# Order of the first loads in a one-token attention and gated-MLP kernel: both halves of the gate weights ahead of the input x

## The chip, the cores and the metric

The kernel runs on one core of a Trainium2 chip. The metric is the device time of one execution in microseconds (us), as the median of several runs. Before the change it is 198.14 us (three runs, 198.09 to 198.21).

The engines named here: TensorE (PE; its weight loads are PEld), VectorE (DVE), ScalarE (ACT), GpSimd (POOL) and SyncE (SP). Transfers between the chip's memory (HBM) and the on-chip SBUF are done by 16 DMA engines. A transfer is put to them by an instruction on SP's queue or on ACT's queue. PSUM is the memory that TensorE writes its sums to.

## What is computed

Eight tokens x (8 x 512, bf16) go through a layer norm. The result feeds an attention over the last 2048 positions of a key and value cache (32 query heads, 8 key/value heads, 128 wide), and a gated MLP that is used as a gate:

```python
xn = _layernorm(x)
# A: attention over the last W = 2048 positions of the caches
q = (xn @ wq), split into 32 heads
p = _softmax(einsum("bhqd,bhkd->bhqk", q, k) * Dh ** -0.5)
s = einsum("bhqk,bhkd->bhqd", p, v) @ wo
# B: the gate
h = _sigmoid(xn @ w_gate) * (xn @ w_up)
g = _silu(h @ w_down)
return x + s * g
```

(The heads' reshapes are left out.) Nearly all the bytes are the two caches, 16 loads of 2 MB each for keys and for values, and the weights: w_gate, w_up and w_down 1.8 MB each, wq and wo 4 MB each; 81 MB in all.

## The kernel before

**Loads.** Nothing is computed without a load, and the loads are put in one long order. A list `todo` holds them with the pool that each needs (k, v or d; L111 to L130), and `pump` (L114) issues from its front as long as the pool has room; `free` (L120), called behind the work that used a tile, gives the room back and issues on. Almost all go on SP's queue (`q0`). In order: `want_first` (L151) with the gate weights and x; w_up (L169); wq in two halves (L205); w_down (L207) and its small remainder `wd_part` in two transfers (L188 to L203); then for each of 16 pairs of token and group of four key heads the keys (from L211) and, three places later, the values; at the end wo in five pieces (L216 to L223). The pool for keys has four tiles, and wq's halves take two of them at first, so the third load of keys waits until the first half of wq has been used. Of `want_first`, four transfers: x as 8 rows of 512 (`x_bf`, L153) on SP's queue; the gate weights (`wg_sb`, L155) in two halves of 896 KB, the first on ACT's queue (`q1`), the second on SP's; and x once more in another layout (`x4_sb`, called x_sb in the profile; L161) on ACT's queue, which is used only at the very end (L770).

A transfer's completion raises one of eight semaphores that the framework hands out in turn, so an issue may wait for the landing of the transfer eight places before it.

**The start.** When x has landed, VectorE casts it to f32 (L228), takes mean and variance (L230, L232), ScalarE takes a square root (L234), VectorE normalises (L237, L239), TensorE transposes the result (L250) and VectorE copies it to `xnT_sb` (L257). Meanwhile GpSimd clears buffers and builds masks and selection matrices (L186, L256 to L323); the largest are two memsets of `qm_sb` (L265). With `xnT_sb`, TensorE computes the two hidden products of the MLP (`hidden`, L327 and L331: gate, then up), a small product with `wd_part`'s selection (L363), and the queries in two halves as wq lands (L416). The queries are spread and transposed (L430 to L455) into `qm_sb`; then w_down is multiplied (L475).

**The main loop** (L687) goes over the 16 pairs: VectorE transposes a tile of keys (L503), TensorE forms the scores (L519, L529), VectorE takes the maximum (L539), ScalarE the exponentials (L571), VectorE transposes them (L582), and TensorE multiplies with the values (L606), four pairs later. Behind the transposes and the products stand the calls of `free` that issue the next loads.

**The end.** The last heads are normalised (L670, L679) and multiplied by wo (L739 for the first 20 rows, L753 for the rest, as they land). Two operations of VectorE (L768, L770) multiply by the gate and add x, and a transfer on SP's queue writes the result (L771).

Of the kernel before, what the change touches and what calls it, by code (L numbers as in the profile page):

```python
# [10 lines left out]
def kernel(  # L11
# [73 lines left out]
    q0, q1 = nc.sync, nc.scalar  # L85
# [55 lines left out]
    x_bf = work.tile([B, D], bf16, name="x_bf")  # L141
# [8 lines left out]

    def want_first():  # L151
        t = vpool.tile([P, KT, F], bf16, name="wg_sb", tag="v")
        q0.dma_start(out=x_bf[:], in_=A_x.flatten_outer_dims())  # L153
        for q, r0 in ((q1, 0), (q0, KT // 2)):
            q.dma_start(  # L155
                out=t[:, r0 : r0 + KT // 2, :],
                in_=B_w_gate.rearrange("(p r) n -> p r n", r=KT)[
                    :, r0 : r0 + KT // 2, :
                ],
            )  # L160
        q1.dma_start(  # L161
            out=x4_sb[::S, :],
            in_=A_x.flatten_outer_dims().rearrange("b (j c) -> j b c", c=P),
        )
        for r in range(KT):
            weights[("wg_sb", r)] = t[:, r, :]

    later("v", want_first)
    want_rows("wu_sb", B_w_up, "v", KT, 0, KT)  # L169

# [45 lines left out]
    for t0, t1, tag in (  # L216
# [18 lines left out]
        out=rstd[:], in_=mv[:, 1:2], func=AF.Sqrt, bias=eps_t[:], scale=1.0  # L235
# [4 lines left out]
        out=xn_bf[:],  # L240
# [8 lines left out]
    for kt in range(KT):  # L249
        nc.tensor.transpose(  # L250
            out=xnT_ps[:, kt, :],
            in_=xn_bf[:].rearrange("b (p kt) -> b kt p", kt=KT)[:, kt, :],
# [11 lines left out]
    for i in range(NQ):  # L264
# [8 lines left out]
        out=mask_rows[:],  # L273
# [10 lines left out]
        out=mask_cols[:],  # L284
        in_=ident[:G, :G].unsqueeze(1).to_broadcast([G, CU * PS, G]),
# [7 lines left out]
    for p0, a, sx in SHARES:  # L293
        n = 4 * a
        nc.gpsimd.tensor_copy(
            out=sel_part[:, :sx, p0 : p0 + n].rearrange("k x (a p) -> k x a p", a=a),
            in_=ident[:, s0 : s0 + n * sx].rearrange(
                "k (p x a) -> k x a p", x=sx, a=a
            ),
# [27 lines left out]
    def hidden(name):  # L327
# [21 lines left out]
        out=h_sb[:].rearrange("k t p -> k p t"),  # L349
# [7 lines left out]
        out=hT_sb[:].rearrange("k t z -> k (t z)"),  # L357
        in_=h_sb[:].rearrange("k t p -> k (t p)"),
# [3 lines left out]
    for x in range(SX):  # L362
# [14 lines left out]
        out=sel_den[:],  # L377
        in_=ident_f[:].rearrange("k (x h) -> k h x", h=GR),
        axis=AX.X,
    )  # L380
    for e in range(2):
        nc.vector.reduce_sum(
            out=sel_out[:, e, :].rearrange("k (i h) -> k i h", i=NQ),
            in_=ident_f[:].rearrange(
                "k (i m e h) -> k e i h m", i=NQ, m=NJ // 2, e=2
            )[:, e],
# [9 lines left out]
        out=sel_res[:],  # L396
# [6 lines left out]
    for i in range(NQ):  # L403
        nc.gpsimd.tensor_copy(
            out=sel_sum[:, i, i],
            in_=sel_den[:].unsqueeze(2).to_broadcast([P, GR, NDQ]),
# [21 lines left out]
    for x in range(NQ):  # L428
        t = ktpool.tile([P, rep * NJE // NE, NE, QS, PG], bf16, name="q_bf", tag="kT")
        move[x](  # L430
            out=t[:],
            in_=q_ps[:, x]
# [5 lines left out]
    for x in range(NQ):  # L438
# [11 lines left out]
        for s in range(QS):  # L450
# [3 lines left out]
                out=qm_sb[x][rows, :, :, o : o + GR].rearrange(  # L454
                    "k y b (l r) -> k y b l r", l=G  # L455
                ),
                in_=qT_ps[rows, x].rearrange("k y r l b -> k y b l r"),
# [305 lines left out]
    for t in range(KS, RT):  # L763
# [8 lines left out]
        out=out.flatten_outer_dims().rearrange("b (j c) -> j b c", c=P),  # L772
        in_=y_bf[::S, :],
# [31 lines left out]
```

## Time and profile before

| What | Value |
|---|---|
| Median of three runs | 198.14 us (198.09 to 198.21) |
| The profiled execution | 198.27 us; its span 196.5 us, and 1.77 us around it |
| Busy: TensorE, VectorE, ScalarE, GpSimd | 138.6, 131.0, 32.4, 11.6 us |
| Bytes moved | 81.19 MB, mean 413 GB/s over the span |
| Packets on SP's queue, on ACT's queue | 6240 (80.10 MB), 180 (0.93 MB) |
| First issue on SP's and on ACT's queue | 0.73 us, 0.74 us |
| Last landing of wo that the chain goes through | 190.84 us |

The span goes from the first to the last instruction, and all times in the timeline are from its start. The page divides the span in 40 slices of 4.9 us: digits are the busy share in tenths; PEclk is the clock granted to TensorE; the DMA row is the mean busy share of the 16 DMA engines. The chain is followed back from the last instruction to what released each step. In the timeline a line is start, duration, engine, source line, operation, written and read tile, and in brackets the idle time before it with what ended it. SPq and ACTq are the queues on which instructions issue transfers; the duration of such a line is that of the issue, not of the transfer. A DMA share can pass 1 in a short window, since a packet is counted where it starts.

### The profile page before, as it was taken

How to read it: one execution, taken by the hardware profiler on the slowest of the kernel's cores; microseconds unless marked ns; L12 is line 12 of the kernel's file. 1: busy time of each engine (PE TensorE's matmuls, PEld its weight loads, DVE VectorE, ACT ScalarE, POOL GpSimd, SP SyncE). 2: the span in 40 equal slices, each digit the busy share in tenths (PEclk: the TensorE clock that was granted, in tenths of full speed). 3: DMA queues.
4: the chain of work that ended last, by engine and by line, in shares of the span. 5: the costliest groups of instructions: out<-in, count | busy, mean ns of one | idle time of the engine just before them, and what ended most of it. 6: DMA issues, size and time to landing. Idle time of an engine off the chain costs nothing.

```text
span 196.5 us, 2541 instructions
## 1 busy us (share of the span) xinstructions
PE 138.6 (71%) x1075; PEld 66.5 (34%) x1075; DVE 131.0 (67%) x144; ACT 32.4 (17%) x62; POOL 11.6 (6%) x31
## 2 busy tenths in 40 slices
PE   0073427846787999699877696995994967998543
PEld 0021121212232553435435252443251624366421
DVE  4617049549799996897775939776649597665101
ACT  0240171000522022020220020220010202210010
POOL 8932000000000000000000000000000000000000
PEclk9999999997999999969999888799699999999985
DMA  6999999999999999999999999999999999999990
GB/s 210 435 435 434 423 430 434 427 434 437 427 430 434 430 427 427 435 424 430 430 430 427 430 435 430 434 427 427 434 434 420 430 434 430 430 430 424 427 381 18
DMA packets 6431, 81.19 MB, mean 413 GB/s; under 512 B 780, under 2 KB 916, under 8 KB 1556
## 3 DMA queue, kind: packets, MB, share of 16 engines
q1 hardware_dynamic: 6240, 80.10, 95.6%
q10 hardware_dynamic: 180, 0.93, 1.5%
q8 instruction: 8, 0.13, 0.2%
q14 instruction: 3, 0.02, 0.0%
HBM read 81.02 MB, written 0.01 MB: 412 GB/s over the span
## 4 chain that ended last, share of the span: by engine, by line
DMA 51%; DVE 23%; PE 21%; ACT 2%; SPq 1%; issue 1%; DVEq 0%; ACTq 0%
DMA k_sb<-in_A_k_cache_dram 29%; DVE kT_sb L503 14%; PE s_ps L529 13%; DMA wo_sb<-in_A_wo_dram 12%; DMA wq_sb<-in_A_wq_dram 10%; DVE st L539 4%; PE o_ps L606 2%; PE s_ps L519 1%; DVE qm_sb L453 1%; DVE pT_sb L582 1%; PE fin_ps L753 1%; ACT qm_sb L453 1%; PE q_ps L416 1%; ACT q_bf L430 1%; PE qT_ps L441 1%
## 5 line engine op out<-in xcount | busy, mean ns | idle before, releaser
L503 DVE STREAM_TRANSPOSE kT_sb<-k_sb 128x2048 f32<-128x2048 f32 x32 | 72.9, 2290 | 5.9 <-DMA k_sb<-in_A_k_cache_dram 5.9
L529 PE MATMUL s_ps<-kT_sb,qm_sb 128*128 128x512 bf16 x256 | 71.6, 426 | 4.7 <-DVE kT_sb L503 4.7
L529 PEld LDWEIGHTS <-qm_sb 128*128 128x128 bf16 x256 | 24.4, 102 | 42.6 <-issue 21.7
L606 PE MATMUL o_ps<-v_sb,pT_sb 128*32 128x256 bf16 x512 | 31.0, 273 | 1.7 <-DMA v_sb<-in_A_v_cache_dram 1.7
L606 PEld LDWEIGHTS <-pT_sb 128*32 128x32 bf16 x512 | 24.4, 97 | 8.4 <-issue 6.5
L539 DVE TENSOR_REDUCE st<-s_ps 128x1 f32<-128x1024 f32 x16 | 19.0, 1190 | 3.9 <-PE s_ps L529 3.9
L568 ACT COPY nb<-m_ps 128x1 f32<-128x1 f32 x16 | 2.5, 159 | 111.6 <-PE m_ps L562 111.6
L544 PE MATMUL m_ps<-ident_f,st 128*1 128x128 f32 x16 | 4.3, 270 | 22.9 <-DVE st L539 22.9
L571 ACT ACTIVATE p_buf<-s_ps,nb 128x1024 bf16<-128x1024 f32 x16 | 17.8, 1115 | 0.5
L519 PE MATMUL s_ps<-mask_cols,mask_rows 4*128 4x512 bf16 x32 | 13.5, 421 | 0.0
L582 DVE STREAM_TRANSPOSE pT_sb<-p_buf 128x512 f32<-128x512 f32 x16 | 11.1, 692 | 0.0
L544 PEld LDWEIGHTS m_ps<-ident_f,st 128*1 128x1 f32 x16 | 1.3, 79 | 27.4 <-DVE st L539 17.3
L670 DVE SCALAR_TENSOR_TENSOR own<-m_ps,inv,own_q 128x128 f32<-128x128 f32 x8 | 2.8, 348 | 10.1 <-PE m_ps L660 8.8
L250 PE MATMUL xnT_ps<-ident,xn_bf 8*128 8x8 bf16 x4 | 0.3, 174 | 10.8 <-POOL fold L316 10.8
L430 DVE CAST q_bf<-q_ps 128x2048 bf16<-128x2048 f32 x1 | 2.3, 2292 | 7.5 <-ACT q_bf L430 7.5
L228 DVE CAST x_f<-x_bf 8x512 f32<-8x512 bf16 x1 | 5.0, 4954 | 2.5 <-DMA x_bf<-in_A_x_dram 2.5
L598 DVE RECIPROCAL inv<-m_ps 128x2 f32<-128x2 f32 x4 | 0.7, 171 | 8.5 <-PE m_ps L590 8.5
L644 DVE TENSOR_TENSOR o_sb<-o_ps,own_col 128x256 f32<-128x256 f32 x8 | 3.1, 385 | 3.7 <-PE o_ps L606 3.7
L660 PE MATMUL m_ps<-o_sb,sel_res 128*128 128x256 f32 (+1 forms) x20 | 4.6, 352 | 1.1 <-DVE o_sb L644 0.5
L562 PEld LDWEIGHTS m_ps<-ident_f,neg 1*128 1x128 f32 x16 | 2.4, 147 | 8.9 <-issue 4.8
L519 PEld LDWEIGHTS <-mask_rows 4*128 4x128 bf16 x32 | 4.0, 126 | 3.6 <-issue 1.7
L416 PE MATMUL q_ps<-wq_sb,xnT_sb 128*32 128x512 bf16 x32 | 3.8, 626 | 2.0 <-DMA wq_sb<-in_A_wq_dram 2.0
(79 smaller groups left out, 76.3 us busy)
## 6 DMA issues: line engine op xcount, KB each, us to landing
k_sb<-in_A_k_cache_dram SPq DMA_DIRECT2D x16, 2048.0 KB, 23.3
v_sb<-in_A_v_cache_dram SPq DMA_DIRECT2D x16, 2048.0 KB, 28.8
wq_sb<-in_A_wq_dram SPq DMA_DIRECT2D x2, 2048.0 KB, 17.0
wu_sb<-in_B_w_up_dram SPq DMA_DIRECT2D x1, 1792.0 KB, 10.6
wd_sb<-in_B_w_down_dram SPq DMA_DIRECT2D x1, 1664.0 KB
wo_sb<-in_A_wo_dram SPq DMA_DIRECT2D x1, 1536.0 KB, 19.7
wo_sb<-in_A_wo_dram SPq DMA_DIRECT2D x1, 1024.0 KB
wg_sb<-in_B_w_gate_dram ACTq DMA_DIRECT2D x1, 896.0 KB
```

Of the source, the lines that this page charges most:

```text
L228: nc.vector.tensor_copy(out=x_f[:], in_=x_bf[:])
L416: nc.tensor.matmul(q_ps[Z * j : Z * (j + 1), x, :], lhsT=xnT_sb[:, kt, :], rhs=weights[("wq_sb", kt)][:, g * rep * Dh : (g + 1) * rep * Dh ...
L430: move[x](out=t[:], in_=q_ps[:, x] .rearrange("k (n m e) -> k n e m", e=NE, m=PG) .unsqueeze(3) .to_broadcast([P, rep * NJE // NE, NE, QS, ...
L503: nc.vector.transpose(out=kT[(t, m)][:] .rearrange("k y c p e -> k c y (p e)") .bitcast(f32), in_=k_sb[:, CM * m : CM * (m + 1), :] .rearr ...
L519: nc.tensor.matmul(s_ps[t][:, m], lhsT=mask_rows[:].rearrange("k x l r -> k (x l r)"), rhs=mask_cols[:].rearrange("k c l -> k (c l)"), sta ...
L529: nc.tensor.matmul(s_ps[t][:, m], lhsT=qm_sb[i][:, y, b, GR * (1 - e) : GR * (1 - e) + P], rhs=keys[:, y // NE, CU * e : CU * (e + 1), :, ...
L539: nc.vector.reduce_max(out=st[t][:], in_=s_ps[t][:].rearrange("k m c -> k (m c)"), axis=AX.X)
L544: nc.tensor.transpose(out=r_ps[t % 2], in_=st.pop(t)[:], identity=ident_f[:])
L571: nc.scalar.activation(out=p_buf[t % 2][:], in_=s_ps.pop(t)[:].rearrange("k m (c e p) -> k (m c) p e", e=2, p=PG), func=AF.Exp, bias=nb[:] ...
L582: nc.vector.transpose(out=pT[t][:].rearrange("k c x e -> k (c x e)").bitcast(f32), in_=p_buf[t % 2][:].rearrange("k c p e -> k (c p e)").b ...
L606: nc.tensor.matmul(o_at[b][32 * k : 32 * (k + 1)].rearrange("k (e d) -> k e d", e=2), lhsT=pT[t][:, (m * CU + c) // 2, :, c % 2], rhs=v[:, ...
L660: nc.tensor.matmul(m_ps[:, x, P : 2 * P], lhsT=sel_res[:].rearrange("k h q -> k (h q)"), rhs=o_of[y][:, x, e, :], start=(e == 0), stop=(e ...
```

## The change

Inside `want_first`, the transfer of `x_bf` on SP's queue is issued behind the loop over the two halves of the gate weights instead of ahead of it. SP's queue now starts with the second half of the gate weights, then x, then w_up as before. ACT's queue keeps its order: the first half, then `x4_sb`. No transfer changes its size, and no other line is touched.

```diff
     def want_first():
         t = vpool.tile([P, KT, F], bf16, name="wg_sb", tag="v")
-        q0.dma_start(out=x_bf[:], in_=A_x.flatten_outer_dims())
         for q, r0 in ((q1, 0), (q0, KT // 2)):
             q.dma_start(
                 out=t[:, r0 : r0 + KT // 2, :],
                 in_=B_w_gate.rearrange("(p r) n -> p r n", r=KT)[
                     :, r0 : r0 + KT // 2, :
                 ],
             )
+        q0.dma_start(out=x_bf[:], in_=A_x.flatten_outer_dims())
         q1.dma_start(
             out=x4_sb[::S, :],
             in_=A_x.flatten_outer_dims().rearrange("b (j c) -> j b c", c=P),
         )
```

## The prediction

> **What bounds the kernel now.** I read the page first: the slices, and the chain that ended last.
>
> ```profile
> PEclk9999999997999999969999888799699999999985
> DMA  6999999999999999999999999999999999999990
> GB/s 210 435 435 434 423 430 434 427 434 437 427 430 434 430 427 427 435 424 430 430 430 427 430 435 430 434 427 427 434 434 420 430 434 430 430 430 424 427 381 18
> ```
>
> From the second slice (4.9 us) to the 38th the DMA engines are full, at about 430 GB/s. Only the first slice (210) and the last two are not. Then the chain in order of time, its end:
>
> ```profile
> 168.00 22.84 DMA wo_sb<-in_A_wo_dram
> 190.84 0.04 issue
> 190.88 1.85 PE fin_ps L753 x41
> ...
> 193.53 0.29 DVE y_bf L770
> ```
>
> The end hangs on the landing of the output weights at 190.84 us, in a transfer issued 22.84 us before: at issue some 22.84 x 0.43 = 9.8 MB stood ahead of it. No engine's work, only the stream itself, decides when it lands. All bytes are the same after the change, so the time moves by what the start of the stream moves, and by how unevenly the 16 DMA engines get through it. So third the start, by the timeline:
>
> ```profile
> 0.73 0.41 SPq L153 DMA_DIRECT2D x_bf<-in_A_x_dram  x1
> 0.74 0.39 ACTq L155 DMA_DIRECT2D wg_sb<-in_B_w_gate_dram  x1
> ...
> 1.20 0.36 SPq L155 DMA_DIRECT2D wg_sb<-in_B_w_gate_dram  x1
> 1.61 0.42 SPq L103 DMA_DIRECT2D wu_sb<-in_B_w_up_dram  x1
> ...
> 2.48 4.95 DVE L228 CAST x_f<-x_bf 8x512 f32<-8x512 bf16 x1 [2.48 <-DMA x_bf<-in_A_x_dram]
> ```
>
> and by the DMA view of the window 2 to 4 us (packets, MB, share of the 16 engines; q10 holds 0.93 MB in the page, ACT's half and the small x4, so it is ACT's queue and q1 is SP's):
>
> ```profile
> q10 hardware_dynamic: 79, 0.57, 80.2%
> q1 hardware_dynamic: 1, 0.00, 0.0%
> ```
>
> SP's half of the gate weights was issued at 1.20, yet up to 4.3 us SP's queue moved nothing of it; its first packets come in 4.4 to 4.5. The engines first work off ACT's half. A view by stage says how busy they are meanwhile (length, then the engines; last the DMA share and GB/s):
>
> ```profile
> 1.75:4.00 2.25, 0.00 (x0) 0.00 (x0) 1.52 (x1) 0.00 (x0) 2.25 (x5) 1.00 0.99 288
> ...
> 5.00:190.00 185.00, 136.32 (x1019) 64.93 (x1019) 127.89 (x142) 32.12 (x62) 7.23 (x19) 0.95 1.01 430
> ```
>
> A share of 0.99 at 288 GB/s: the DMA engines are occupied, but their first packets are slow. In 1.5 to 2 us eleven of ACT's packets take 120.2% of 16 engines for 0.5 us, 9.6 / 11 = 0.87 us each; in 4 to 4.4 us 24 take 102.6%, 0.27 us each. Two alone in windows of 0.01 us (1.885 and 1.895) show 800.0% and 875.0%: 1.28 and 1.40 us. The ramp costs (430 - 288) x 2.25 / 430 = 0.74 us.
>
> **The change, part by part.**
>
> *SP's half goes from second to first on its queue.* Its issue moves from 1.20 to 0.73, 0.47 us earlier (the 0.41 us of x and a gap). What that is worth lies between 0.47 and nothing: the engines were occupied with ACT's packets until 4.3 us, and one packet at a time is served per engine (share near 1), so an earlier half only takes the place of the other. What remains is the first packet. SP's queue moved its first at 1.65 to 1.70 (x, issued at 0.73), ACT's its first at 1.78 to 1.79, ten more by 2.0. A half on SP's queue at 0.73 should start where x started, 0.09 us before ACT's. I take -0.09 us.
>
> The Trainium skill, page "DMA: Bandwidth & Descriptors", section "Issuing engines are not separate DMA queues", says that transfers issued from several engines run on the same DMA engines, and that issuing from several saves only the sequencer's issue time. Read as the whole of that issue time, it would give -0.47, rival A below; the row above (nothing moved of a half issued at 1.20) says that even this saving finds the engines taken.
>
> *x goes behind 896 KB.* Its transfer moves from a time when nothing else runs into the full stream. Seven of its packets in 1.70 to 1.75 take 35.2%: 0.352 x 16 x 0.05 / 7 = 0.04 us each, one on each of up to eight engines. Cost: between 0 (if the engine that finishes last has none) and 0.05 with its completion write. I take +0.05. x is issued at about 1.14 instead of 0.73, and wu still at 1.61, as the two issues only swap.
>
> *x lands later, and what waits.* It landed at 2.48. Behind its half it lands, by the ends known, between 4.6 (SP's half first on every engine, as ACT's now) and 7.9 us (SP's half's landing now, 1.20 + 6.7). Who waits: the cast at L228, then L230 to L257, then TensorE. But the cast's 4.95 us is no work of its own. GpSimd runs without a gap beside it, and the cast ends 0.28 us after GpSimd's last big memset:
>
> ```profile
> 5.14 2.01 POOL L265 MEMSET qm_sb<- 128x2304 uint32 x1
> ```
>
> 5.14 + 2.01 = 7.15; 2.48 + 4.95 = 7.43. A DVE operation of the same 8x512 (L239) takes 0.54. So up to a landing at 7.1 the cast still ends at 7.43; at 7.9 it ends at 8.2 to 8.5, or near 9.1 if it is held until the small gap in GpSimd's row at 8.84. That is 0 to 1.7 us on the path to the query. The next row hides it:
>
> ```profile
> 21.98 1.90 PE L416 MATMUL q_ps<-wq_sb,xnT_sb 128*32 128x512 bf16 x16 [2.03 <-DMA wq_sb<-in_A_wq_dram]
> ```
>
> TensorE stands 2.03 us there until the second half of wq lands; a delay below 2.03 is gone by 21.98. And if that cover went, the stream has its own: the third k load, issued at 19.99 when a slot comes free, has 13.6 thousand KB (13.9 MB) queued ahead; with 0.65 MB moved by 4.0 us, they last to 4 + 13.25 / 0.43 = 34.8 us, 14.8 us after that issue. The end sees nothing. Cost 0.
>
> *SP's own waits.* The issues of wd_part and the first k load wait for an earlier transfer's landing (SP's waits: 1.7 us for wg at L194, 0.2 at L93), as a transfer's completion semaphore is shared with the eighth after it. With the order of the first ones changed they wait for halves that land by about 7 to 8 instead of 5.9 and 7.9: up to 2 us later for wd_part, and behind it k loads; 9.6 MB are queued ahead of them, until 4 + 8.9 / 0.43 = 24.7 us. Cost 0.
>
> Sum: -0.09 + 0.05 = -0.04 us. The profiled execution lasted 198.27 us (span 196.5 and 1.77 around it), so 198.23 by that; against the median of 198.14 it is 0.13 high, and the forecast for the median is **198.1 us**. The tail does not alter this: TensorE works through L753 at half clock (0.50 from 190 us) from one landing on, and shifts with it.
>
> **Rivals.**
>
> *A: the second stream fills the ramp.* If two halves at once hide each other's slow first packets, the issue time counts in full: 198.14 - 0.47 = 197.67; no more than the ramp's 0.74 (197.40) is there to win. For it: 0.74 us is lost there. Against: the engines are occupied (0.99), and SP's half did not slip in while ACT's packets crawled. 0.16.
>
> *B, slower: another engine is last.* The engines do not end together: the share falls to 0.92, 0.56 and 0.04 in the three us from 190, so a transfer is landed by the last of them, and a delay that one picks up at the start stays with it. Two first packets took 1.28 and 1.40 us against a mean of 0.87. With both queues' packets starting at once the slow ones can fall on the engine that is last anyway. Price: 1.40 - 0.87 = 0.53, 198.1 + 0.53 = 198.6; it decides once the last engine's lag grows by over 0.4. The small x packets on the lower engines push the same way. The same draw can win as much, if the present last one was the 1.40. 0.15 for the loss.
>
> *C: it does not do what it says.* If ACT's half still comes first on every engine, SP's goes exactly when it goes now and only x is late: 198.14 + 0.05 = 198.2. It counts with the forecast, within 0.2%.
>
> A late x that reaches the end (it would need a landing some 15 us later) has 0.01.
>
> **From cases to numbers.** 0.2% is 0.4 us, about what a measurement of this kernel can tell from no change. Forecast and C hold 0.68 (within 197.74 to 198.54), A and a lucky draw of B 0.16 (faster), B and the late x 0.16 (slower). The range takes A's 197.67 and B's 198.6: 197.65 to 198.65.
>
> **What the changed profile would show.** SP's queue moves packets of the gate weights from 1.7 us, before or beside ACT's; GB/s of 1.75 to 4 stays near 288 (A: above 350). The cast at L228 starts between 4.6 and 8 and takes under 3 us; its end moves by less than 2. TensorE still waits for wq at L416, a shorter wait if x is later. All slices from the second stay full, and the wo landing moves with the first packet. I am wrong if the ramp is filled, if the last landing moves by more than 0.4 against the stream's start, or if a slice in the middle shows a gap.

## The result and the profile after

The change makes the kernel slower by 0.47 us: 198.61 us median (198.29 to 198.82, 18 runs) against 198.14 (197.96 to 198.34, 18 runs), a ratio of 1.0022, 95% interval 1.0015 to 1.0028. The forecast was 198.1. The profiled execution of the changed kernel lasted 198.40 us, only 0.13 more than that of before (198.27); a second profile of the same kernel, taken beside the experiments and called *after2* here, lasted 198.73, 0.46 more. Both are read below, since one execution alone would show too little.

The slices of the page of after:

```profile
DMA  6999999999999999999999999999999999999990
GB/s 198 438 434 430 426 438 423 433 427 430 430 430 433 430 443 427 428 420 440 427 427 427 433 428 430 433 430 433 430 433 430 427 433 427 427 420 436 426 382 19
```

The DMA engines are full in the same slices as before, so nothing inside the stream has changed. What differs is the first slice, 198 for 210 GB/s. The timeline of after, the first issues and the cast:

```profile
0.73 0.39 SPq L154 DMA_DIRECT2D wg_sb<-in_B_w_gate_dram  x1
0.74 0.40 ACTq L154 DMA_DIRECT2D wg_sb<-in_B_w_gate_dram  x1
...
1.18 0.37 SPq L160 DMA_DIRECT2D x_bf<-in_A_x_dram  x1
1.59 0.35 SPq L103 DMA_DIRECT2D wu_sb<-in_B_w_up_dram  x1
...
8.02 0.88 DVE L228 CAST x_f<-x_bf 8x512 f32<-8x512 bf16 x1 [8.02 <-DMA x_bf<-in_A_x_dram]
```

The halves are now issued 0.01 us apart instead of 0.46. x lands at 8.02 instead of 2.48; the cast takes 0.88 us instead of 4.95 and ends at 8.90 instead of 7.43. The wait that was to hide this, by the timeline of TensorE in after:

```profile
22.11 1.90 PE L416 MATMUL q_ps<-wq_sb,xnT_sb 128*32 128x512 bf16 x16 [1.11 <-DMA wq_sb<-in_A_wq_dram]
```

TensorE still waits for the second half of wq, 1.11 us where it was 2.03: the late x is used up there. The product starts 0.13 us later than before (22.11 against 21.98) because that half lands later. Now the start by the DMA view of after, window 2 to 4 us (packets, MB, share of the 16 engines; q1 is SP's queue, q10 ACT's):

```profile
q1 hardware_dynamic: 34, 0.24, 39.3%
q10 hardware_dynamic: 35, 0.25, 30.7%
```

Before, ACT's half had these 2 us to itself (79 packets to 1). Now the queues share them, and together move 69 packets where 80 were moved. The Trainium skill, page "DMA: Bandwidth & Descriptors", section "Queues, rings and completion order", says that a DMA engine takes its queues in turn; this trace agrees with it (34 to 35), that of before, where ACT's queue alone was served until 4.3 us though SP's half had been issued at 1.20, shows no such turns. By stage, the last three us of before (length, the engines, DMA share and GB/s last):

```profile
190.00:191.00 1.00, 0.12 (x8) 0.12 (x12) 0.00 (x0) 0.31 (x1) 0.00 (x0) 0.50 0.92 373
191.00:192.00 1.00, 1.00 (x32) 0.89 (x29) 0.00 (x0) 0.00 (x0) 0.00 (x0) 0.50 0.56 219
192.00:193.00 1.00, 0.98 (x32) 0.56 (x23) 0.00 (x0) 0.00 (x0) 0.00 (x0) 0.50 0.04 14
```

the start and the last three us of after:

```profile
1.75:4.00 2.25, 0.00 (x0) 0.00 (x0) 0.00 (x0) 0.00 (x0) 2.25 (x5) 1.00 0.97 258
...
190.00:191.00 1.00, 0.00 (x1) 0.00 (x1) 0.00 (x0) 0.43 (x1) 0.00 (x0) 0.72 0.92 373
191.00:192.00 1.00, 1.00 (x32) 0.92 (x33) 0.00 (x0) 0.00 (x0) 0.00 (x0) 0.50 0.62 244
192.00:193.00 1.00, 0.99 (x32) 0.63 (x24) 0.00 (x0) 0.00 (x0) 0.00 (x0) 0.50 0.10 37
```

and the same of after2:

```profile
1.75:4.00 2.25, 0.00 (x0) 0.00 (x0) 0.00 (x0) 0.00 (x0) 2.25 (x5) 1.00 0.95 261
...
190.00:191.00 1.00, 0.17 (x4) 0.00 (x0) 0.00 (x0) 0.59 (x1) 0.00 (x0) 0.56 0.91 369
191.00:192.00 1.00, 0.61 (x24) 0.61 (x28) 0.00 (x0) 0.00 (x0) 0.00 (x0) 0.50 0.65 258
192.00:193.00 1.00, 1.00 (x34) 0.78 (x25) 0.00 (x0) 0.00 (x0) 0.00 (x0) 0.50 0.15 55
```

The ramp (1.75 to 4 us) is slower, 258 and 261 GB/s against 288; that is (288 - 258) x 2.25 / 430 = 0.16 and 0.14 us of the full rate. What is left to move after 190 us, the sum of the last three shares, is 0.92 + 0.62 + 0.10 = 1.64 us of all engines in after and 0.91 + 0.65 + 0.15 = 1.71 in after2, against 1.52 before: the engines are behind by 0.12 and 0.19 us on the mean. The DMA view counts the same in bytes. Up to 4 us, before and then after:

```profile
DMA packets 106, 0.65 MB, mean 163 GB/s; under 512 B 8, under 2 KB 16, under 8 KB 106
DMA packets 81, 0.58 MB, mean 145 GB/s; under 512 B 0, under 2 KB 0, under 8 KB 81
```

and up to 188 us:

```profile
DMA packets 5981, 79.74 MB, mean 424 GB/s; under 512 B 690, under 2 KB 826, under 8 KB 1111
DMA packets 5972, 79.69 MB, mean 424 GB/s; under 512 B 689, under 2 KB 825, under 8 KB 1105
```

After is 0.07 MB behind at 4 us and 0.05 MB at 188, which is 0.16 and 0.12 us at 430 GB/s: the lag is there by 4 us and stays. The end follows the last of them, by the chain of after and then of after2:

```profile
169.19 21.76 DMA wo_sb<-in_A_wo_dram
191.00 1.86 PE fin_ps L753 x46
```

```profile
171.26 20.08 DMA wo_sb<-in_A_wo_dram
191.39 2.26 PE fin_ps L753 x47
```

The landing that the end waits for comes at 190.95 and 191.34 us instead of 190.84: 0.11 and 0.50 us later, about as much as the 0.13 and 0.46 by which these executions are longer. Of after2's half microsecond 0.19 is the mean lag of all engines; the other 0.3 would then be one or a few engines that are further behind than the rest.

### The profile page after: what moved, and what is told of

Same layout as the page of the kernel before. It is cut to its first block, busy times and chain, and to the rows that moved or that the text cites. A ratio compares the mean times of both kernels' runs of the same rounds, so it can differ in the third digit from the quotient of the medians.

```text
span 196.6 us, 2527 instructions
## 1 busy us (share of the span) xinstructions
PE 135.8 (69%) x1061; PEld 66.5 (34%) x1075; DVE 126.9 (65%) x144; ACT 32.4 (16%) x62; POOL 11.5 (6%) x31
## 4 chain that ended last, share of the span: by engine, by line
DMA 50%; DVE 23%; PE 20%; ACT 2%; issue 1%; SPq 1%; DVEq 0%; ACTq 0%
DMA k_sb<-in_A_k_cache_dram 29%; DVE kT_sb L503 14%; PE s_ps L529 13%; DMA wo_sb<-in_A_wo_dram 11%; DMA wq_sb<-in_A_wq_dram 10%; DVE st L539 4%; PE o_ps L606 2%; DVE qm_sb L453 1%; DVE pT_sb L582 1%; PE s_ps L519 1%; PE fin_ps L753 1%; ACT qm_sb L453 1%; SPq L103 1%; PE q_ps L416 1%; ACT q_bf L430 1%
## 5 line engine op out<-in xcount | busy, mean ns | idle before, releaser
L529 PE MATMUL s_ps<-kT_sb,qm_sb 128*128 128x512 bf16 x242 | 69.0, 429 | 7.3 <-DVE kT_sb L503 4.7
L519 PE MATMUL s_ps<-mask_cols,mask_rows 4*128 4x512 bf16 x32 | 13.0, 407 | 0.0
L228 DVE CAST x_f<-x_bf 8x512 f32<-8x512 bf16 x1 | 0.9, 879 | 8.0 <-DMA x_bf<-in_A_x_dram 8.0
L546 DVE TENSOR_REDUCE top<-m_ps 1x16 f32<-1x128 f32 x16 | 4.0, 252 | 1.3 <-PE m_ps L544 1.2
```

Source lines behind the costliest of these rows:

```text
L519: nc.tensor.matmul(s_ps[t][:, m], lhsT=mask_rows[:].rearrange("k x l r -> k (x l r)"), rhs=mask_cols[:].rearrange("k c l -> k (c l)"), sta ...
L529: nc.tensor.matmul(s_ps[t][:, m], lhsT=qm_sb[i][:, y, b, GR * (1 - e) : GR * (1 - e) + P], rhs=keys[:, y // NE, CU * e : CU * (e + 1), :, ...
L546: nc.vector.reduce_max(out=top[:], in_=r_ps[t % 2].rearrange("o (x h) -> o h x", h=GR), axis=AX.X,)
```

## The experiments

Three theories stood at first. T1: two large transfers that start at once hinder each other. T2: a small transfer ahead of a large one on its queue makes it start quickly, and the change takes that away. T3: the late x reaches the end after all. Each ratio is against before, run on the same chip beside the kernel (medians 198.06 us beside a to d, 198.13 beside after2 and e to g, 198.10 beside i, h and b1, 198.06 beside k, o and m). The diffs are cut down to the order of issues in `want_first`, or to the line that is added ahead of it; "first half" and "second half" are those of the gate weights.

### One stream, and x late or early

```diff
 # a_serial_x_last
-q0: x;  q1: first half;  q0: second half;  q1: x4
+q0: first half, second half, x;  q1: x4
 # b_serial_x_act
+q1: x;  q0: first half, second half;  q1: x4
```

> Both halves of the gate weights on SP's queue, x behind them, ACT's queue with x4 alone. Three theories of the 0.47 us that the change costs. T1, two streams at once: the first packets of two large transfers hinder each other, so the ramp is slower (258 instead of 288 GB/s from 1.75 to 4 us). Here there is one stream: about 198.1 us, 1.75 to 4 us at 285 GB/s or more. T2, x as a primer: a small transfer ahead of the large one on its queue makes the large one's first packets quick. Here none stands ahead of it: 198.6. T3, late x: x lands at about 6.5 to 7 us, far behind the 2.48 of before, and the delay of the queries reaches the end: 198.4 to 198.6.

> Both halves on SP's queue, x first on ACT's queue, x4 behind it. T1 (two streams): 198.1 or a little less, since one stream starts at 0.73 and the small transfers run while it starts. T2 (primer on the same queue): 198.6, as nothing small stands ahead of the weights on SP's queue. T3 (late x): x is early, about 2.5 us, so 198.1.

a: 198.15 us, ratio 1.0007 (0.9998 to 1.0016). b: 197.97, 0.9996 (0.9987 to 1.0004). The timeline of a has

```profile
8.00 0.89 DVE L228 CAST x_f<-x_bf 8x512 f32<-8x512 bf16 x1 [8.00 <-DMA x_bf<-in_A_x_dram]
```

x is as late as in the change (8.00 against 8.02), and nothing clear of the noise is lost (at most 0.3 us by the interval): T3 falls, and k below, where x is late too, bears it out. Nothing small stands ahead of SP's large transfer, in a nor in b: T2 falls for a single stream. The ramp is 299 GB/s in a and 279 in b.

### Small transfers ahead

```diff
 # c_swap_small
+q0: x4;  q1: first half;  q0: second half, x
 # d_x_split_first
+q0: x rows 0-3;  q1: x rows 4-7;  q1: first half;  q0: second half;  q1: x4
```

> x4 first on SP's queue, then its half, then x; ACT's queue starts with its half as before. ACT's half has the DMA engines to itself at the start, and x is as late as in the change (near 8 us). T1 (two streams): 198.1, 1.75 to 4 us at about 288 GB/s. T2 (primer): 198.1. T3 (late x): 198.6.

> x early and both halves at once: four rows of x first on each queue, then a half on each, both issued at about 1.2 us. The stream starts 0.45 us later than before for that reason alone: 198.14 + 0.45 = 198.6. T1 (two streams): the loss comes on top, 198.6 + 0.47 = 199.05, with SP's and ACT's packets mixed from the start. T2 (primer) and T3 (late x): 198.6.

c: 198.74 us, 1.0034 (1.0023 to 1.0046). d: 198.63, 1.0029 (1.0017 to 1.0040). c is slow as T3 gave, but not by its way: its ramp is good (303 GB/s), and it loses from 4 to 10 us, where it moves 405 and then 415 GB/s (4 to 7, 7 to 10 us) and before 440 and 428; that is 0.33 of its 0.68 us. Its halves are issued 1.02 us apart, so by T1 it should have lost nothing, and T1 missed it. Why it loses is not settled. d is what its later start was to give, so no loss on top is seen, and T1's 199.05 was missed too; but its halves were issued 0.17 us apart (1.18 and 1.35), not at once. It is inconclusive.

### The change again, and both halves apart in time

```diff
 # after2: the change
+q1: first half;  q0: second half, x;  q1: x4
 # e_mirror
+q1: x;  q0: second half;  q1: first half, x4
 # f_act_later
+q1: x4;  q0: second half;  q1: first half;  q0: x
 # g_x_pool: the change, x on GpSimd's queue
+nc.gpsimd: x;  q1: first half;  q0: second half;  q1: x4
```

> The change once more, beside the others on the same chip: 198.5 to 198.7, slower than before by 0.4 to 0.6 us by every theory; 1.75 to 4 us at 230 to 265 GB/s by T1 (two large transfers at once), and a last landing later than before by about what that ramp leaves behind.

> SP's queue: its half, nothing ahead and x not behind it. ACT's queue: x, then its half some 0.6 us later, then x4. x is early. T1 (two large transfers started at once hinder each other): they no longer start at once, so 198.0 to 198.2. T2 (a large transfer with nothing small ahead of it on its queue starts slowly): SP's half has nothing ahead, 198.5 or more. T3 (late x): x early, 198.1; but the run with one stream and x at 8.0 us gave 198.15, so T3 is no longer believed.

> The change with one difference: on ACT's queue x4 stands ahead of its half, so the half is issued about 1.3 us later than SP's. x is as late as in the change. T1 (at once): 198.1 to 198.2. T2 (nothing small ahead of SP's half) and T3 (late x): 198.6.

> Both halves at once as in the change, each first on its queue, but x is issued on GpSimd's queue and lands early. T1 (at once): 198.5 to 198.7, with both queues' packets mixed from 2.5 us. T3 (late x): 198.1. GpSimd's own work starts some 1 us later by the issue, which by the run with late x should not reach the end.

after2: 198.53 us, 1.0015 (1.0006 to 1.0024). e: 198.15, 1.0001 (0.9992 to 1.0009). f: 198.18, 1.0005 (0.9997 to 1.0014). g: 198.68, 1.0028 (1.0016 to 1.0039). With 0.66 us (e) or 1.40 us (f) between the issues of the halves, SP's first, the loss is gone; with both at 0.74 (g) it is there. The ramp alone does not say so: it is 292 and 303 GB/s in e and f, and in g 277, near the 279 of b, which loses nothing. g's premise failed: GpSimd issued x only at 3.05, behind its memsets, and it landed at 9.07, so g does not part T1 from T3. f's x landed at 5.38, so f does not either; a does.

### A distance of 0.1 us, another tensor, one transfer

```diff
 # i_offset: the change, and ahead of it
+wg_t = vpool.tile(...); nc.gpsimd.memset(wg_t[0:1, KT // 2, 0:2], 0.0)
 # h_other_tensor: the change, but SP's first is half of w_up
+q1: gate rows 0-1;  q0: up rows 0-1, x, gate rows 2-3, up rows 2-3;  q1: x4
 # b1_single: as b, the gate weights in one transfer
+q1: x;  q0: all gate rows;  q1: x4
```

> The change, its order of issues kept, but SP's half waits for a memset of two elements by GpSimd that is over at about 0.95 us, so that it is issued some 0.2 us behind ACT's half and not 0.01 us before it. Nothing small stands ahead of either half, and x is late. T1 (at once): 198.1 to 198.3, no first packet over 1.5 us. If it is only that two large transfers run side by side without a small one ahead: 198.6.

> At once as in the change, but SP's first transfer is half of the up weights and not the other half of the gate weights; the second halves of both follow behind x on SP's queue. If the loss comes from starting two large transfers at once (T1), whatever they read: 198.5 to 198.7, with some first packets of 1.7 us or more. If it comes from both reading neighbouring rows of the same tensor: 198.1 to 198.2.

> The whole gate weights in one transfer of 1792 KB on SP's queue, x first on ACT's queue and x4 behind it. By T1 one large transfer starts alone: 197.9 to 198.1, as with two halves one behind the other on SP's queue (197.97). Packets are twice as large (14336 B), so the first ones may be slower; that would show as 198.2.

i: 198.51 us, 1.0021 (1.0010 to 1.0031). h: 198.76, 1.0035 (1.0024 to 1.0047). b1: 198.58, 1.0022 (1.0013 to 1.0031). The memset in i was over sooner than meant, and SP's half was issued at 0.85, 0.11 us behind ACT's: by its time that is still at once. By its timeline, and by stage:

```profile
0.74 0.43 ACTq L156 DMA_DIRECT2D wg_sb<-in_B_w_gate_dram  x1
0.85 0.39 SPq L156 DMA_DIRECT2D wg_sb<-in_B_w_gate_dram  x1
```

```profile
1.75:4.00 2.25, 0.00 (x0) 0.00 (x0) 0.00 (x0) 0.00 (x0) 2.25 (x5) 1.00 0.81 252
```

The time that T1 gave (198.1 to 198.3) was missed, and the other one (198.6) came, because 0.11 us are not enough; k decides between the two. The ramp is slower than that of the change, but not by slow packets: the slowest first one takes 1.27 us, and at a share of 0.81 the DMA engines stand idle for a fifth of the time. h loses as much as the change though the two transfers read different tensors, so neighbouring rows are not the cause; its slowest first packet takes 1.46 us, below the 1.7 expected. b1 was missed: one stream, and yet 0.48 us slower, at 283 GB/s on the ramp, with first packets (of 14336 B) of up to 1.88 us. T1 does not explain it.

### The distance of before without anything small ahead; packet sizes

```diff
 # k_offset45: as i, with a larger memset
+nc.gpsimd.memset(wg_t[:, KT // 2, 0:400], 0.0)
 # o_double: the change with transfers of 1792 KB
+q1: all gate rows;  q0: all up rows, x;  q1: x4
 # m_quarters: as b, the gate weights in four transfers
+q1: x;  q0: gate row 0, 1, 2, 3;  q1: x4
```

> The change with SP's half held by a memset of GpSimd in its rows until about 1.2 us: its issue then stands some 0.45 us behind ACT's, as it stood before the change behind x, but nothing small is ahead of either half and x is still behind. T1 (at once, within about 0.1 us): 198.1 to 198.25. If a small transfer has to stand ahead (T2), or if the late x counts beside large transfers on two queues: 198.5 to 198.7.

> The suspected cost doubled: at once on both queues, but transfers of 1792 KB with packets of 14336 B (ACT the whole gate weights, SP the whole up weights), x behind. If the price is slow first packets met by both queues (T1), it grows with the packet: 198.9 to 199.3, first packets above 2 us. If the packet's size is nothing: 198.5 to 198.7.

> The other way: one stream on SP's queue as in the run with both halves there (197.97), but in four quarters of 448 KB, so that the first packets are 3584 B; x first on ACT's queue. If slow first packets set what an engine falls behind by, smaller ones cost less: 197.7 to 197.95. If not: 198.0 to 198.1.

k: 198.03 us, ratio 1.0000 (0.9991 to 1.0009). o: 198.42, 1.0018 (1.0010 to 1.0027). m: 199.46, 1.0068 (1.0055 to 1.0082). k is the change in all but the time between the two issues and what follows from it: SP's later issues come 0.45 us later too. (Their time is not what counts: e issues w_up earlier than before, at 1.18, and loses nothing either.) By its timeline

```profile
0.74 0.39 ACTq L156 DMA_DIRECT2D wg_sb<-in_B_w_gate_dram  x1
...
1.19 0.39 SPq L156 DMA_DIRECT2D wg_sb<-in_B_w_gate_dram  x1
1.64 0.35 SPq L162 DMA_DIRECT2D x_bf<-in_A_x_dram  x1
...
7.68 0.48 DVE L230 CAST x_f<-x_bf 8x512 f32<-8x512 bf16 x1 [7.68 <-DMA x_bf<-in_A_x_dram]
```

x is still behind its half and late (7.68). In its window of 2 to 4 us ACT's queue is alone again, and its ramp and its end are better than before's:

```profile
q10 hardware_dynamic: 80, 0.57, 75.4%
```

```profile
1.75:4.00 2.25, 0.00 (x0) 0.00 (x0) 0.00 (x0) 0.00 (x0) 2.18 (x7) 1.00 1.00 303
...
192.00:193.00 1.00, 0.81 (x24) 0.34 (x15) 0.12 (x1) 0.00 (x0) 0.00 (x0) 0.50 0.01 2
```

So 0.45 us between the issues, with nothing small ahead and x late, is enough to lose nothing: T2 falls, and T1 holds in this, that starting at once costs. That it costs by slower first packets and a slower ramp does not hold everywhere: i has no slow packet, and o loses 0.36 us with a ramp of 306 GB/s and a slowest first packet of 1.68 us (above 2 was expected). o and m are misses for the thought that slow first packets cost by their size: doubled packets at once cost no more than single ones (o), and halved ones in one stream cost 1.4 us (m). Most of m's loss is in a second slow stretch of its own:

```profile
4.00:7.00 3.00, 0.00 (x0) 0.00 (x0) 3.00 (x1) 0.00 (x0) 3.00 (x2) 1.00 0.94 285
```

Its four issues of the gate weights last until 2.85 us, that of w_up ends at 3.33, and from 4 to 7 us its engines move 285 GB/s where before moved 440, which is (440 - 285) x 3 / 430 = 1.08 us. Why is not shown.

## Why the prediction was wrong

**The step that failed** is "SP's half goes from second to first on its queue". It was bounded by a gain of 0.47 and by nothing, with -0.09 taken, because "an earlier half only takes the place of the other": a loss was left out of the bounds. Its measure is +0.47 us, the difference of the medians; all else that the change does is in k as well (k adds a memset), and k costs nothing (0.9991 to 1.0009). The row that I read, engines occupied at a share of 0.99, was right. The reasoning from it was not: that a second stream can't help busy engines does not mean that it can't hurt them. Before had never shown two large streams starting together, so no row excluded a loss.

**Rival B** had the time (198.6) and the place, the engine that is last. Single packets of the first ones, in windows of after2 (start 1.855 and 1.875, 0.01 us long; packets, MB, share):

```profile
q1 hardware_dynamic: 1, 0.01, 1318.1%
```

```profile
q1 hardware_dynamic: 1, 0.01, 1280.6%
```

These are 13.18 x 16 x 0.01 = 2.11 and 2.05 us for one packet, where the slowest before was 1.40; in after one takes 1.83 us. B had the old packets fall on another engine; in after and after2 they became slower instead. That B's number was met is in part luck: its 0.53 was the spread of before's first packets, and i and h lose 0.41 and 0.66 us with no first packet above 1.27 and 1.46. That the engines with the slow packets are the last at 190 us is argued, not shown: no view names the engine of a packet.

**Rival A** is rejected: the ramp is 258 and not above 350 GB/s. **C** falls too: SP's packets do come first; from 1.5 to 2 us twelve of them start and none of ACT's.

**The first packet** was to come 0.09 us earlier. SP's queue moved nothing from 1.65 to 1.75, its first packets start in 1.75 to 1.80: by these windows the large transfer starts 0.05 to 0.15 us later than the small x did (1.65 to 1.70), and against ACT's first packet before (1.78 to 1.79) the gain was 0.04 us at most.

**x behind 896 KB** held in the main: landing at 8.02, just past the upper end of 4.6 to 7.9; the cast under 3 us (0.88) and its end 1.47 us later (below 2); the wait for wq smaller and not gone. That this costs the end nothing clear of noise is shown by a and k; the term of +0.05 is too small for any run here to tell.

**SP's waits** were mis-sized, and free as said: the first transfer of wd_part is issued at 8.33 instead of 5.87 and the first k load at 11.28 instead of 7.93, where up to 2 us was said. The latter waits for the landing of x4, which I had not named. The slices show no gap, and e and f issue their first k load later still (12.75 and 13.69) and lose nothing.

**The chances**: 0.16 stood on slower by over 0.2%; the median lies at 0.24%, just past that bound, and inside the range only because B's price was taken into it.

## What stays open

That the distance between the two issues makes the loss is shown; by what steps is not. Slower first packets are seen in after, after2 and g (1.83, 2.11 and 1.81 us), not in i and h; a slower ramp in after, after2, h and i, hardly in g, not in o; each of these is one profiled execution. h rules out only that neighbouring rows are the cause. That one or a few engines fall behind the rest is argued from the shares. Where between 0.11 and 0.45 us the cost ends is open, as d (0.17) starts later for another reason. b1, one stream with packets of 14336 B, loses 0.48 us, c loses behind the ramp, and m in 4 to 7 us; none of these is explained by T1. No version beats both kernels: the best, b, has an interval that includes 1.

## What to carry to other kernels

Where a kernel is bound by its stream of transfers from the first microsecond, the end moves with the start: here by what the DMA engines had moved less by 4 us, and, as is argued, by how far the last of them falls behind there. Try such a kernel with its two large first transfers not started on two queues at the same moment; half a microsecond between them, here the issue of a small transfer that is wanted early anyway, cost nothing in before and k. It is no safe rule: c keeps its halves apart and is slower for another reason. And when a price is bounded from rows in which the situation never occurs, leave the other sign inside the bounds.

## What the runs showed of the hardware

Two transfers of 896 KB or more, the first on their queues and issued 0 to 0.11 us apart, cost 0.36 to 0.66 us by the medians in six runs of five kernels (after, after2, g, h, i, o: ratios of 1.0015 to 1.0035). Two issued 0.45 us apart or more cost nothing in e, f and k against before, which has them 0.46 us apart; c, 1.02 us apart, loses 0.68 us for a reason that is open, but is not behind at 4 us (0.68 MB against before's 0.65). The Trainium skill, page "DMA: Bandwidth & Descriptors", section "Issuing engines are not separate DMA queues", says of issuing from several engines that it only saves the time of issue; here it can also cost. And what the ramp leaves behind (0.16 and 0.14 us in after and after2) is still there at 190 us (0.12 and 0.19): the full stream between, at 430 GB/s, did not make it up.
